# Recurrent attention in steps of 64 tokens of two batches instead of 128 tokens of one, with transposed outputs

## The chip, the cores and the metric

The kernel runs on one NeuronCore of one Trainium2 chip. Four of the core's engines matter here: TensorE (PE in the profile, with the loading of its weights as PEld), VectorE (DVE), ScalarE (ACT) and GpSimd (POOL); SyncE (SP) gives out the DMA transfers. The metric is the device time of one execution in microseconds. The kernel before was timed in three runs: 598.31, 598.85 and 598.88 us, so the median is 598.85 us.

## The reference

A gated linear attention over 4 batches of 8 heads, 768 tokens, with heads of 48 channels, is followed by a feed-forward layer:

```python
for t in range(S):                                    # S = 768
    state = alpha[:, :, t, :, None] * state + einsum('bhd,bhe->bhde', k[:, :, t], v[:, :, t])
    y[:, :, t] = einsum('bhd,bhde->bhe', q[:, :, t], state)
x = y.transpose(0, 2, 1, 3).reshape(B * S, H * D)     # 3072 x 384
h = x @ w_in                                          # 384 x 2048
g = h * erf(softplus(h))
out = g @ w_out                                       # 2048 x 384, result 3072 x 384
```

All data are float32. The state of a head is a 48x48 matrix; row d of it is multiplied by alpha[d] at every token.

## The kernel before

**Tiling.** The 3072 tokens are 24 chunks of 128 tokens, each of one batch, so six chunks follow each other in a batch and hand on the state. Two chunks are a block of 256 tokens, and there are 12 blocks. A chunk goes through the steps ld, a1 to a6, a block through H, L1, L2, E, Z, O and out. Heads are kept in pairs: channels of an even head lie in partitions 0 to 47, those of the odd head of the pair in 64 to 111, and four pairs lie side by side. The 16 partitions behind each head hold fixed filling (ones for alpha, zeros for q and k).

**A chunk.** `ld` (line 130) issues seven DMAs on SP's queue: two each for alpha, k and q, one for v. alpha, k and q go to three fixed tiles, of which there is one set. `a0` (line 139) has ACT look for large alphas. `a1` (line 143) runs four scans on DVE, one for each pair, which give the running product A of alpha within the chunk, and POOL copies its last column to `ae`. `a2` has ACT form 1/A by Ln and Exp, in PSUM, and DVE refine it; `a3` multiplies k by 1/A (K) and q by A (Q). `a4` (line 168) multiplies K by Q on PE, one 48x128x128 product for each of eight heads (`pS`, L174); DVE masks the upper triangle (`sT`, two operations, L180). PE also transposes K (`pn`, L187), and ACT copies that (`kn`). `a5` (line 193) adds up the output `py`: Q times the state T for each pair (L199, where the chunk is not the first of its batch) and the masked scores times v for each head (L205). If the chunk is not the last of its batch, the products of K and v follow (`pu`, L214), and DVE updates T (L224 to L229) by four operations on 64 partitions. `a6` (line 231) turns the output, which has tokens in its partitions, into x, which has channels there: three transposes on PE (`px`, L254), a copy on ACT to `x_hi` (L256) and the rest of float32 on DVE as `x_lo` (L257).

**A block.** `H` (line 259) multiplies x by w_in, 18 matrix products for each half of a group (three for each product of float32 parts: `x_hi` and `x_lo` by `wi_hi`, `x_hi` by `wi_lo`); ACT takes the result out of PSUM twice (L283, L284). `L1`, `L2`, `E` and `Z` compute the activation on ACT and DVE; `O` (line 311) splits it into two parts (L320 to L323) and multiplies by w_out (L331), 12 products for each half of a group; `out` writes 256 rows.

**Weights.** 28 steps `wi` and `wo` load the weights as float64 words, turn these into float32 and split them in two parts, on ACT and DVE (L360 to L368, L343, L344). They are all in the first part of the program.

**What sets the order.** Three lists at the top (START, ORDER, TAIL) give the steps in an order written out by hand: START with the weights and the first chunks, ORDER once for each block in between, TAIL at the end. In ORDER the step `a6_0` ends a block's x, and `H_0_0@1` and `H_0_1@1` come right behind it, ahead of `L2_0`, `L2_1` and the four steps `O_2_0@-1` to `O_3_1@-1`. From the order of the steps the framework's planner makes a fixed sequence of instructions for each engine and for SP's queue: it takes the first instruction in the list's order whose inputs should be there by its own costs, so instructions of neighbouring steps interleave. At run time each engine works its sequence in order.

Buffers: PSUM has four banks for attention (`ps_at`), two for H (`ps_h`) and two for the accumulators.

## Time and profile before

| what | value |
|---|---|
| median of three runs | 598.85 us (598.31 to 598.88) |
| span of the profiled execution, first to last instruction | 594.3 us |
| PE busy | 552.4 us (93%), 4282 products |
| DVE busy | 503.0 us (85%), 769 instructions |
| ACT busy | 485.1 us (82%), 845 instructions |
| POOL busy | 20.9 us (4%), 40 instructions |
| DMA engines, mean over the span | 62 GB/s, 20220 packets |

For the profiled execution the profile gives its span; the time of that execution outside the span is not listed by itself, and the median of the runs is 4.55 us above the span. Busy times of PE overlap within one engine since products are pipelined; the interval from one product's start to the next one's is the price of a product in a row of them. A float32 product stands in the profile as two instructions, each with a weight load of its own; a product of the shortened kind (`x_hi`, `wo_hi` and so on) and a transpose stand as one. In a row of a group, "48\*128 48x128" is rows by columns of the weights, and then partitions by elements of what is streamed.

### The profile page before, as it was taken

What the parts mean: (1) busy time and instruction counts of PE and PEld (TensorE: products, weight loads), DVE (VectorE), ACT (ScalarE), POOL (GpSimd) and SP (SyncE); (2) the same over time, 40 slices, a digit from 0 to 9 for tenths busy, and PEclk for the clock granted to TensorE, in tenths of its full rate; (3) what the DMA queues carried; (4) which work ended last, traced back from release to release, by engine and by line L of the source; (5) the groups of instructions that cost most, each with busy time, mean ns of one, the idle gap of its engine ahead of it and who ended that gap; (6) DMA issues with size and microseconds to landing.
All of it is one profiled execution on the core that took longest, in us unless ns stands there. A gap on an engine that the chain in (4) does not pass through costs nothing.

```text
span 594.3 us, 11033 instructions
## 1 busy us (share of the span) xinstructions
PE 552.4 (93%) x4282; PEld 534.8 (90%) x4282; DVE 503.0 (85%) x769; ACT 485.1 (82%) x845; POOL 20.9 (4%) x40
## 2 busy tenths in 40 slices
PE   0679798999999999999999999999999999999994
PEld 0568787999999999999999999999999999999884
DVE  7899999999999869869779879879779879758780
ACT  4558979698989879889879879889788888889941
POOL 1000110002000000000000000000000000000000
PEclk9999798998999999999999999999999999999998
DMA  6584312313112102112112102112112101000001
GB/s 196 176 290 145 110 55 81 120 54 94 28 41 81 41 26 68 41 29 68 40 28 68 41 28 67 41 39 70 28 35 66 34 28 41 1 1 28 1 27 33
DMA packets 20220, 36.98 MB, mean 62 GB/s; under 512 B 3520, under 2 KB 9664, under 8 KB 20160
## 3 DMA queue, kind: packets, MB, share of 16 engines
q1 hardware_dynamic: 20160, 36.19, 19.9%
q8 instruction: 36, 0.59, 0.4%
q14 instruction: 24, 0.20, 0.1%
HBM read 31.46 MB, written 4.72 MB: 61 GB/s over the span
## 4 chain that ended last, share of the span: by engine, by line
PE 81%; DVE 9%; ACT 6%; DMA 2%; issue 1%; SPq 0%; ACTq 0%; DVEq 0%
PE acc L331 33%; PE ph L272 30%; PE py L205 7%; PE pS L174 4%; PE py L199 3%; PE pu L214 2%; DMA wst<-in_moe_w_in_dram 2%; PE pn L187 1%; PE px L254 1%; DVE hs L309 1%; DVE s L308 1%; DVE A L146 1%; ACT wbuf L360 1%; ACT w L283 1%; DVE wbuf L365 1%
## 5 line engine op out<-in xcount | busy, mean ns | idle before, releaser
L272 PE MATMUL ph<-x_hi,wi_hi 128*128 128x256 f32 x576 | 164.0, 288 | 4.0 <-ACT hs L284 3.4
L272 PE MATMUL ph<-x_lo,wi_hi 128*128 128x256 f32 x576 | 163.4, 284 | 0.4 <-DVE x_lo L257 0.4
L272 PE MATMUL ph<-x_hi,wi_lo 128*128 128x256 f32 x576 | 163.2, 284 | 0.0
L331 PE MATMUL acc<-wo_hi,gh 128*128 128x384 f32 x384 | 134.5, 351 | 3.6 <-DVE gh L320 2.6
L331 PE MATMUL acc<-wo_lo,gh 128*128 128x384 f32 x384 | 131.3, 342 | 0.0
L331 PE MATMUL acc<-wo_hi,gl 128*128 128x384 f32 x384 | 130.0, 344 | 1.2 <-DVE gl L323 1.2
L272 PEld LDWEIGHTS ph<-x_hi,wi_hi 128*128 128x128 f32 x576 | 110.4, 192 | 5.8 <-ACT hs L284 4.2
L272 PEld LDWEIGHTS ph<-x_lo,wi_hi 128*128 128x128 f32 x576 | 110.5, 192 | 0.7 <-DVE x_lo L257 0.7
L272 PEld LDWEIGHTS ph<-x_hi,wi_lo 128*128 128x128 f32 x576 | 110.5, 192 | 0.5 <-DVE wi_lo L344 0.5
L283 ACT ACTIVATE w<-ph 128x512 f32<-128x512 f32 x96 | 57.5, 599 | 46.9 <-PE ph L272 44.0
L297 DVE TENSOR_TENSOR t<-s,w 128x1024 f32<-128x1024 f32 x48 | 58.5, 1219 | 29.4 <-ACT w L291 29.3
L331 PEld LDWEIGHTS acc<-wo_hi,gh 128*128 128x128 f32 x384 | 72.8, 190 | 5.3 <-DVE gh L320 2.6
L331 PEld LDWEIGHTS acc<-wo_hi,gl 128*128 128x128 f32 x384 | 72.2, 190 | 2.6 <-DVE gl L323 2.6
L323 DVE TENSOR_TENSOR gl<-hs,gh 128x512 fp32r<-128x512 f32 x96 | 65.3, 683 | 10.8 <-ACT gh L322 10.3
L331 PEld LDWEIGHTS acc<-wo_lo,gh 128*128 128x128 f32 x384 | 73.2, 191 | 0.0
L205 PE MATMUL py<-raw_v,sT 128*128 128x48 f32 x384 | 57.9, 279 | 5.5 <-DVE sT L180 5.5
L308 DVE TENSOR_TENSOR s<-s,w 128x1024 f32<-128x1024 f32 x48 | 58.2, 1218 | 2.3 <-ACT s L303 2.1
L205 PEld LDWEIGHTS py<-raw_v,sT 128*128 128x128 f32 x384 | 53.8, 203 | 6.8 <-DVE sT L180 6.6
L298 DVE SCALAR_TENSOR_TENSOR w<-t,w 128x1024 f32<-128x1024 f32 x48 | 58.4, 1217 | 0.4
L309 DVE SCALAR_TENSOR_TENSOR hs<-s,hs 128x1024 f32<-128x1024 f32 x48 | 58.2, 1217 | 0.3
L289 ACT ACTIVATE s<-w,fixed 128x1024 f32<-128x1024 f32 x48 | 55.1, 1151 | 0.0
L284 ACT ACTIVATE hs<-ph 128x512 f32<-128x512 f32 x96 | 54.8, 593 | 0.0
(67 smaller groups left out, 834.2 us busy)
## 6 DMA issues: line engine op xcount, KB each, us to landing
wst<-in_moe_w_in_dram SPq DMA_DIRECT2D x12, 512.0 KB, 4.6
wst<-in_moe_w_out_dram SPq DMA_DIRECT2D x16, 384.0 KB, 3.4
raw_a<-in_alpha_dram SPq DMA_DIRECT2D x48, 96.0 KB, 2.2
raw_k<-in_k_dram SPq DMA_DIRECT2D x48, 96.0 KB, 2.2
raw_q<-in_q_dram SPq DMA_DIRECT2D x48, 96.0 KB, 2.2
raw_v<-in_v_dram SPq DMA_DIRECT2D x24, 192.0 KB, 2.4
out_dram<-o SPq DMA_DIRECT2D x24, 192.0 KB, 1.9
```

Of the source, the lines that this page charges most:

```text
L174: nc.tensor.matmul(out=pss[par][:, pair, :], lhsT=self.K[rows, pair, :], rhs=self.Q[rows, pair, :], start=True, stop=True,)
L205: nc.tensor.matmul(out=py[:, h * D : (h + 1) * D], lhsT=self.sT[par][:, pair, :], rhs=vt[:, h, :], start=self.first, stop=self.first or pa ...
L272: nc.tensor.matmul(out=o, lhsT=wt[:, kt, fs], rhs=xt[:, kt, :], start=n == 0, stop=n == 3 * KT - 1)
L283: tab(nc.scalar.activation(w, ph, AF.Exp, accum_out=self.pl.flags[:, n : n + 1]))
L284: nc.scalar.activation(self.hs[g][:, sl], ph, AF.Copy)
L289: tab(nc.scalar.activation(s, w, AF.Ln, bias=bone))
L297: nc.vector.tensor_tensor(out=t, in0=s, in1=w, op=ALU.mult)
L298: nc.vector.scalar_tensor_tensor(out=w, in0=t, scalar=2.0, in1=w, op0=ALU.subtract, op1=ALU.mult)
L308: nc.vector.tensor_tensor(out=s, in0=s, in1=w, op=ALU.mult)
L309: nc.vector.scalar_tensor_tensor(out=h, in0=s, scalar=RT2 / 2, in1=h, op0=ALU.add, op1=ALU.mult)
L323: nc.vector.tensor_tensor(out=gl.rearrange("p a t -> p (a t)"), in0=gg, in1=ghf.bitcast(F32), op=ALU.subtract)
L331: nc.tensor.matmul(out=self.acc[tt][:, :DM], lhsT=gt[:, u, ts], rhs=wt[:, f, :], start=f == 0 and n == 0, stop=f == NF - 1 and n == 2,)
```

## The change

A step (still called a chunk) now takes 64 tokens of two batches: `NI = 2` streams of `TC = 64` tokens. There are still 24 of them, but 12 follow each other for each of two pairs of batches, so 2 of the 24 are the first of a batch and 2 the last (before: 4 and 4). The lists START, ORDER and TAIL are not changed.

- Loads: two sets of tiles for alpha, k and q, and two buffers for v. Four more DMAs for each chunk load v a second time (`vx`), so that the two heads of a pair lie in the two halves of the partitions; each of these moves 64 partitions x 4 x 48 floats. POOL clears `vx`'s last 16 columns.
- `a1`: one scan over all 512 columns. It has to start anew at each of the eight pieces of 64: POOL copies the first factor of each piece to a tile `lower`, clears that factor in the data rows (two memsets, one for each head's 48 partitions), and the scan's second operand (max with `lower`) puts the value back.
- `a2`: 1/A is formed in SBUF, w and K share a tile; the look for large values is made here, on A.
- `a4`: the transposes of K come first. The scores are 16 products of 48x64 by 64, whose results lie in one bank, the even head's in partitions 0 to 63, the odd head's in 64 to 127. One masking operation.
- `a5`: the output comes transposed, channels in partitions: 16 products with the state as weights (48x64) and 16 with `vx` as weights (64x64), in the order state, vx for the even head, then state, vx for the odd head. The products of K and v are 16, of 64 rows and 64 columns, and lie in two banks, one for each stream. T is one tile for both streams; DVE updates it by three operations (one where the chunk is the first: two).
- `a6`: no transposes. Every second chunk, six DMAs on SP's queue move rows from one place of the output tile `xf` to another (the fourth pair's channels fill the 16 partitions behind each head of the other three; `w_in`'s rows are put in the same order on the host), and then one copy on ACT and one subtraction on DVE over 768 columns give `x_hi` and `x_lo`.

```diff
-    for nm, fill in (("a", 1.0), ("q", 0.0), ("k", 0.0)):
-        t = raw.tile([P, NP, P], F32, name=f"raw_{nm}")
-        nc.vector.memset(t, fill)
-        raws.append(t)
+    for n in range(2):
+        ra, rq, rk = (raw.tile([P, NP, NI, TC], F32, name=f"raw_{nm}{n}") for nm in "aqk")
+        for t, fill in ((ra, 1.0), (rq, 0.0), (rk, 0.0)):
+            (nc.vector if n == 0 else nc.gpsimd).memset(t, fill)
+        raws.append((ra, rq, rk))
...
         def ld(self):
-            self.vt = raw.tile([P, H, D], F32, name="raw_v", tag="raw_v")
+            self.vt = raw.tile([P, H * D], F32, name="raw_v", tag="raw_v", bufs=2)
+            self.vx = raw.tile([P, NI * NP * D + HD - D], F32, name="raw_x", tag="raw_x", bufs=2)
+            nc.gpsimd.memset(self.vx[:, NI * NP * D :], 0.0)
...
+            for par in range(2):
+                for i in range(NI):
+                    nc.sync.dma_start(
+                        out=self.vx[par * HD : (par + 1) * HD, i * NP * D : (i + 1) * NP * D].rearrange(
+                            "t (a d) -> t a d", a=NP
+                        ),
+                        in_=v[self.m, self.c, i * TC : (i + 1) * TC, :].rearrange(
+                            "t (a b d) -> t b a d", a=NP, b=2
+                        )[:, par],
+                    )
...
         def a1(self):
+            first = self.ra[:, :, :, 0]
+            nc.gpsimd.tensor_scalar(
+                out=lower[:, :, :, 0], in0=first, scalar1=AMIN, scalar2=None, op0=ALU.max
+            )
+            for par in range(2):
+                nc.gpsimd.memset(first[par * HD : par * HD + D], 0.0)
+            nc.vector.tensor_tensor_scan(
+                out=self.A.rearrange(flat), data0=self.ra.rearrange(flat), data1=lower.rearrange(flat), initial=1.0,
+                op0=ALU.mult, op1=ALU.max,
+            )
...
         def a4(self):
+            ps = ps_at.tile([P, NP * NI, TC], F32, name="pS", tag="at")
             for pair in range(NP):
+                for i in range(NI):
+                    for par in range(2):
+                        rows = slice(par * HD, par * HD + D)
+                        nc.tensor.matmul(
+                            out=ps[par * HD : (par + 1) * HD, pair * NI + i, :],
+                            lhsT=K[rows, pair, i, :], rhs=Q[rows, pair, i, :], start=True, stop=True,
+                        )
...
+        def a5(self, moe):
             for pair in range(NP):
+                for i in range(NI):
+                    at0 = (i * NP + pair) * D
+                    for par in range(2):
+                        o = py[par * HD : (par + 1) * HD, pair * NI + i, :]
+                        if not self.first:
+                            nc.tensor.matmul(
+                                out=o, lhsT=T[par * HD : par * HD + D, at0 : at0 + HD],
+                                rhs=self.Q[par * HD : par * HD + D, pair, i, :], start=True, stop=False,
+                            )
+                        nc.tensor.matmul(
+                            out=o, lhsT=vx[par * HD : (par + 1) * HD, at0 : at0 + HD],
+                            rhs=self.sT[par * HD : (par + 1) * HD, pair * NI + i, :], start=self.first, stop=True,
+                        )
             if not self.last:
+                pu = [ps_at.tile([P, 512], F32, name="pu", tag="at") for _ in range(NI)]
                 for pair in range(NP):
                     for par in range(2):
+                        for i in range(NI):
+                            toks, h = slice(i * TC, (i + 1) * TC), 2 * pair + par
+                            nc.tensor.matmul(
+                                out=pu[i][par * HD : (par + 1) * HD, pair * D : (pair + 1) * D],
+                                lhsT=self.kn[toks, pair, par, :], rhs=vt[toks, h * D : (h + 1) * D],
+                                start=True, stop=True,
+                            )
+            nc.scalar.activation(
+                moe.xf[:, :, :, s, :].rearrange("p a i t -> p (a i) t"), py, AF.Copy,
+            )
...
         def a6(self, moe):
             if self.n % 2 == 0:
-                moe.alloc_x()
-            moe.turn(self.yt.rearrange("p a b d -> p (a b d)"), self.n % 2, ps_at, "at")
+                return
+            for j in range(KT):
+                for par in range(2):
+                    nc.sync.dma_start(
+                        out=xf[par * HD + D : (par + 1) * HD, j, :],
+                        in_=xf[par * HD + j * G : par * HD + (j + 1) * G, NP - 1, :],
+                    )
+            moe.alloc_x()
+            x_hi, x_lo = moe.x
+            nc.scalar.activation(x_hi, xf[:, :KT, :], AF.Copy)
+            nc.vector.tensor_tensor(out=x_lo, in0=xf[:, :KT, :], in1=x_hi.bitcast(F32), op=ALU.subtract)
```

Blocks keep 256 tokens, 128 of each of the two batches, so H, L, E, Z and O are not changed, and `out` writes to two places. The path for inputs that the fast way can't carry (`general`) follows the new layout; no instruction of it stands in the profile before.

More of the change, by code (lines that the diff above doesn't have):

```diff
@@ L193, in a5 @@
[L193 to L211 removed]
+                    nc.sync.dma_start(out=t[par * HD : par * HD + D], in_=src[self.m, self.c, par])
@@ new lines, in a3, with a4 @@
+        def a3(self):
+            flat = "p a i t -> p (a i t)"
+            w = self.K.rearrange(flat)
+            nc.vector.tensor_tensor(out=w, in0=self.rk.rearrange(flat), in1=w, op=ALU.mult)
+            self.Q = at.tile([P, NP, NI, TC], F32, name="Q", tag="Q")
+            nc.vector.tensor_tensor(
+                out=self.Q.rearrange(flat), in0=self.rq.rearrange(flat), in1=self.A.rearrange(flat), op=ALU.mult
+            )
+        def a4(self):
+            K, Q = self.K, self.Q
+            if not self.last:
+                pn = ps_at.tile([P, 512], F32, name="pn", tag="at")
+                for pair in range(NP):
+                    nc.tensor.transpose(
+                        pn[:, pair * P : (pair + 1) * P], K[:, pair].rearrange("p i t -> p (i t)"), ident
+                    )
+                self.kn = at.tile([P, NP, 2, HD], F32, name="kn", tag="kn", bufs=1)
+                nc.scalar.activation(self.kn.rearrange("p a b d -> p (a b d)"), pn, AF.Copy)
+            ps = ps_at.tile([P, NP * NI, TC], F32, name="pS", tag="at")
+            for pair in range(NP):
+                for i in range(NI):
[5 more added lines that the diff above has]
+                        )
+            self.sT = at.tile([P, NP * NI, TC], F32, name="sT", tag="sT", bufs=1)
+            nc.vector.tensor_tensor(
+                out=self.sT, in0=ps, in1=maskn.unsqueeze(1).broadcast_to([P, NP * NI, TC]), op=ALU.mult
+            )
@@ L223, in a5 @@
+            nc.scalar.activation(
+                moe.xf[:, :, :, s, :].rearrange("p a i t -> p (a i) t"), py, AF.Copy,
+            )
+            if not self.last:
+                aeb = self.ae.unsqueeze(3).broadcast_to([P, NI, NP, D])
+                for i in range(NI):
+                    U = pu[i][:, : NP * D].rearrange("p (a d) -> p a d", a=NP)
                     if self.first:
                         nc.vector.scalar_tensor_tensor(
-                            out=Tp, in0=Up, scalar=-1.0, in1=ap, op0=ALU.mult, op1=ALU.mult
+                            out=Tv[:, i], in0=U, scalar=-1.0, in1=aeb[:, i], op0=ALU.mult, op1=ALU.mult
@@ L246, in alloc_x, with order @@
             self.x = (x_hi, x_lo)
+        def order(self, y):
+            t = self.pl.gp.tile([P, KT, 2, HD], F32, name="yo", tag="yo", bufs=1)
+            pairs = y.rearrange("p (a b d) -> p a b d", a=NP, b=2)
+            nc.vector.tensor_copy(out=t[:, :, :, :D], in_=pairs[:, :KT])
+            for j in range(KT):
+                G = HD - D
+                nc.vector.tensor_copy(out=t[:, j, :, D:], in_=pairs[:, NP - 1, :, j * G : (j + 1) * G])
+            return t.rearrange("p j b d -> p (j b d)")
         def turn(self, y, c, pool, tag):
@@ L420, in general @@
                     nc.sync.dma_start(
[L421 removed]
+                        out=part[g, b, bass.ds(c * TC, TC), :, par, :].rearrange("t a e -> a t e"), in_=gy[r : r + NP]
                     )
@@ L452, in gla_moe @@
     new_phase(LNEXP)
-    chunks = [Chunk(n) for n in range(2 * NBLK)]
-    moes = [Moe(i * TB, pools) for i in range(NBLK)]
+    chunks = [Chunk(n) for n in range(NS)]
+    moes = []
+    for n in range(NBLK):
+        m, j = divmod(n, CPB // 2)
+        moes.append(Moe(n, [(m * NI + i) * S + j * P for i in range(NI)], pools))
     def run(order, c0, b0):
@@ L517 @@
     from concourse.bass_utils import run_bass_kernel_spmd as _run
-    nc = _bacc.Bacc("TRN2", target_bir_lowering=False, num_devices=1)
+    nc = _bacc.Bacc("TRN2", target_bir_lowering=False, num_devices=1, dynamic_dma_scratch_size=2048)
     arrays, args = {}, []
     B, H, S, D = inputs["q"].shape
-    P = 128
-    CPB = S // P
+    NI, TC, NP, DM = 2, 64, H // 2, H * D
+    M, C, G = B // NI, S // TC, 64 - D
+    order = [
+        c
+        for j in range(NP - 1)
+        for par in range(2)
+        for c in (
+            *range((2 * j + par) * D, (2 * j + par + 1) * D),
+            *((2 * NP - 2 + par) * D + j * G + z for z in range(G)),
+        )
+    ]
     for name in _INS:
```

180 lines of the change are left out of this document (70 added, 110 removed).

## The prediction

> **What bounds the kernel now.** I read the page's busy times and its chain of waits first, then busy time by stretches, then the chain in order of time.
>
> ```profile
> PE 552.4 (93%) x4282; PEld 534.8 (90%) x4282; DVE 503.0 (85%) x769; ACT 485.1 (82%) x845; POOL 20.9 (4%) x40
> PE 81%; DVE 9%; ACT 6%; DMA 2%; issue 1%; SPq 0%; ACTq 0%; DVEq 0%
> ...
> 0.00:100.00 100.00, 68.73 (x509) 62.20 (x510) 92.27 (x178) 72.51 (x138) 8.89 (x22) 0.95 0.49 152
> 332.50:377.30 44.80, 44.80 (x369) 43.88 (x368) 38.03 (x57) 38.14 (x67) 0.83 (x2) 1.00 0.15 45
> ```
>
> The columns of the last two rows are the stretch, then busy time of PE, PEld, DVE, ACT and POOL, the granted clock, the DMA share and GB/s. Averages mislead: in the first 100 us DVE is the busy one (92 of 100 us, PE 69), and in a block of the middle PE has no gap at all while DVE and ACT stand at 38 of 44.8 us. So a microsecond off PE's work counts from about 100 us on, and a microsecond off DVE before that.
>
> ```profile
> 245.34 1.09 PE pS L174 x16
> ...
> 288.10 1.09 PE pS L174 x16
> ...
> 332.90 1.09 PE pS L174 x16
> 338.81 2.12 PE acc L331 x12
> 340.92 2.14 PE ph L272 x18
> ...
> 377.68 1.09 PE pS L174 x16
> ```
>
> From the chain: a block takes 377.68 - 332.90 = 44.8 us, and one with a last and a first chunk of a batch 288.10 - 245.34 = 42.8 us, so such a boundary saves 2.0 us. H takes 144 x 2.14/18 = 17.1 us of a block and O 96 x 2.12/12 = 17.0 us. Attention has the other 10.7 us, 5.3 us for a chunk, and only this part is changed.
>
> ```profile
> 332.83 1.16 PE L174 MATMUL pS<-Q,K 48*128 48x128 f32 x16
> 333.92 0.66 PE L187 MATMUL pn<-ident,K 128*128 128x128 f32 x4
> 334.33 0.36 PE L272 MATMUL ph<-x_hi,wi_hi 128*128 128x256 f32 x1
> ...
> 342.90 0.36 PE L199 MATMUL py<-T,Q 128*128 128x96 f32 x2
> ...
> 345.61 0.67 PE L214 MATMUL pu<-raw_v,kn 128*64 128x48 f32 x16
> 346.21 0.44 PE L331 MATMUL acc<-wo_hi,gh 128*128 128x384 f32 x1
> ...
> 346.67 0.49 PE L254 MATMUL px<-ident,y 128*128 128x128 f32 x3
> 346.91 0.42 PE L331 MATMUL acc<-wo_hi,gl 128*128 128x384 f32 x1
> ```
>
> From start to start in PE's timeline: scores 1.09 us, transposes of K 0.41, output 2.71, K times v 0.60, transposes of the output 0.24; together 5.05 us.
>
> **PE, part by part.** The new forms are 64x64 and 48x64 weights in quarters of the array; no row shows one. The nearest rows are the weight loads:
>
> ```profile
> 332.83 0.19 PEld L174 LDWEIGHTS pS<-Q,K 48*128 48x128 f32 x2
> 332.83 0.97 PEld L174 LDWEIGHTS pS<-Q,K 48*128 48x128 f32 x16
> 345.02 0.53 PEld L205 LDWEIGHTS py<-raw_v,sT 128*128 128x128 f32 x4
> 345.61 0.55 PEld L214 LDWEIGHTS pu<-raw_v,kn 128*64 128x64 f32 x16
> ...
> L214 PEld LDWEIGHTS pu<-raw_v,kn 128*64 128x64 f32 x320 | 11.7, 146 | 1.2
> ```
>
> Output: 4 loads of 128 columns in 0.53 us, one of which lasts 0.19, so three steps of 0.113 us; that is the pace of the whole group, since only 48 or 96 elements are streamed against each. Scores: 16 loads of 128 columns, 15 steps in 0.97 - 0.19, 0.052 us each: these alternate between the upper and the lower half of the rows, and two go on at once. Their first row says more: two loads start within 0.01 us. The source puts both instructions of the even head's product ahead of the odd head's, and one place needs 0.11 us for each, so the second to start is the odd head's, ahead of its turn. Each half works through a stream of its own. K times v: 64 columns, 15 steps in 0.55 - 0.15 = 0.40, 0.027 us each; with the two halves of the columns in turn that is 0.055 us for a load in one place, half of 0.11 for half the columns.
>
> I take it that quarters too are streams of their own, 0.055 us for an instruction in each. *Scores:* 32 instructions in two quarters, 16 x 0.055 = 0.88; the old 1.09 held 8 x 0.105 = 0.84 and 0.25 of entering and leaving, so 1.13. *Transposes of K:* 0.41 as before, now ahead of the scores. *Output:* 64 instructions in two quarters, 32 x 0.055 = 1.76, and 0.10 for entering: 1.86 for 2.71. Four instructions now follow each other in one quarter, not two. If PE looked ahead by less than that, three of four would be paid in full: 16 x 3 x 0.055 = 2.64, no gain; the loads that overtake speak for the lower value. *K times v:* 32 instructions. In four quarters 8 x 0.055 = 0.44 and 0.16 at the edges, 0.60 as before; if only two run at once, 1.04. I take four, since row halves and column halves are each seen side by side. *Transposes of the output:* 0.24 gone. Sum 4.00, which is 1.05 us less for a chunk.
>
> How many chunks count? The masking stands behind each pair of score groups:
>
> ```profile
> L180 DVE TENSOR_TENSOR sT<-pS,maskn x10: 680/684/692, 21.7 to 92.0; 128x512 f32<-128x512 f32 x10
> L180 DVE TENSOR_TENSOR sT<-pS,maskn x38: 660/680/693, 110.1 to 511.8; 128x512 f32<-128x512 f32 x38
> ```
>
> 5 chunks up to 100 us and 19 after, by two a chunk. 19 x 1.05 = 20.0 us saved. Of this goes back what the batches' edges saved: before, three last and three first chunks after 100 us, 6.0 us; now one first (without the state's products, 0.88) and two last (without 0.41 and 0.60), 2.9 us. That is 3.1 lost, 16.9 us net.
>
> **DVE, ACT and POOL.**
>
> ```profile
> L146 DVE TENSOR_TENSOR_SCAN A<-raw_a,fixed 128x128 f32<-128x128 f32 x96 | 35.1, 406 | 0.0
> L180 DVE TENSOR_TENSOR sT<-pS,maskn 128x512 f32<-128x512 f32 x48 | 30.9, 679 | 0.4 <-PE pS L174 0.4
> L257 DVE TENSOR_TENSOR x_lo<-px,x_hi 128x384 fp32r<-128x384 f32 x24 | 13.4, 557 | 11.3 <-ACT x_hi L256 10.5
> L229 DVE TENSOR_TENSOR T<-T,ae 64x192 f32<-64x192 f32 x32 | 11.3, 353 | 0.8
> L209 ACT ACTIVATE y<-py 128x384 f32<-128x384 f32 x24 | 11.8, 490 | 14.3 <-PE py L205 14.3
> L155 ACT ACTIVATE r<-A 128x512 f32<-128x512 f32 x24 | 14.4, 599 | 1.9 <-DVE A L146 1.9
> 334.62 0.19 POOL L151 COPY ae<-A 128x4 f32<-128x4 f32 x1 [22.56 <-DVE A L146]
> 73.43 3.04 POOL L151 COPY ae<-A 128x4 f32<-128x4 f32 x1 [9.16 <-DVE A L146]
> ```
>
> DVE for a chunk: one masking less, 0.68; four state operations of 0.35 become two of the same length and one of 384 columns (0.56 by `x_lo`'s row), 0.15 less; one scan for four, nothing to 0.2; half of two `x_lo` merged, nothing to 0.1. Together 0.8 to 1.1 us. ACT: the output copy has 512 columns like 1/A's Ln, 0.11 more; the rest is even. In the middle neither is on the path. Up to 100 us, five chunks give 4 to 5.5 us back where DVE waits for nothing. Against this stand three POOL operations ahead of each scan. The copy of 128x4 took 0.19 us beside an easy DVE and 3.04 us in the stretch where DVE was full, but if DVE itself stands waiting for POOL, POOL has it free: 3 x 0.2 to 0.6 for a chunk, at most 3 us over five. The second set of tiles lets POOL begin while the scan before is being used. The four extra DMAs cost SP's queue:
>
> ```profile
> 356.15 0.78 SPq L136 DMA_DIRECT2D raw_a<-in_alpha_dram  x2
> raw_a<-in_alpha_dram SPq DMA_DIRECT2D x48, 96.0 KB, 2.2
> ```
>
> 0.39 us of SP for one, 2.2 us to landing. Five chunks x 4 x 0.39 = 7.8 us of SP in the first 100 us, ahead of weights, partly where nothing waits; loads that waited for the single tiles start earlier. For the start I take 3 us gained, bounds 7 gained and 6 lost.
>
> **The moved step: from output to x.** Before:
>
> ```profile
> 345.71 0.49 ACT L209 ACTIVATE y<-py 128x384 f32<-128x384 f32 x1 [0.95 <-PE py L205]
> 347.19 0.49 ACT L256 ACTIVATE x_hi<-px 128x384 fp32r<-128x384 f32 x1
> 348.05 0.40 PE L272 MATMUL ph<-x_hi,wi_hi 128*128 128x256 f32 x2
> ```
>
> From the end of the output products (345.61) to H on the new x: 2.4 us. Now: copy 0.6, six issues on SP 6 x 0.39 = 2.3, landing 2.2, one copy of 768 columns up to 0.98, handing on 0.4, so 6.5 us, 4 us more in each of 12 blocks. The work that hides it is O of the block before (four steps of 12 products, 8.5 us, behind H in the list), the next chunk's scores, and L2's DVE work. Behind the waiting `x_hi` on ACT stand copies out of PSUM for which PE waits; behind the six DMAs on SP stand the next loads and `out`, which have time. Cover gone altogether: 12 x 4 = 48 us. The planner fills by its own costs, so I take half a microsecond for a block, 6 us.
>
> **Sum.** Against the profiled execution: 594.3 - 16.9 - 3 + 6 = 580.4 us of span; the runs' median is 4.55 us above that span, and so 585 us.
>
> **Rivals.** *Two quarters at a time, or a part of the gain lost among DVE and ACT:* K times v costs 0.44 more, 19 x 0.44 = 8 us, 593. ACT at 38.1 of a block of 43 us would be 89% busy, which leaves waits little room; PE's full rows speak against more than that.
>
> *The wait for x takes over (slower):* with the same PE gain, the block's H stands for the moved rows. It decides from (16.9 + 3)/12 = 1.7 us unfilled in each block; at 2.5 us it costs 30 for my 6, so 609 us. For it: SP gives out six transfers one by one, in a fixed order, and DVE and ACT queue behind. Against it: 8.5 us of O to fill with.
>
> *Quarters take turns (slower):* the quarters of one product pair write to one bank, and in rows 0 to 63 and 64 to 127 nothing shows that two may do so at once; the old scores wrote to two banks. Then scores cost 32 x 0.055 + 0.25 = 2.0 and the output 64 x 0.055 + 0.10 = 3.6, with 0.41 and 0.60 6.6 us, 1.6 more than now: 19 x 1.6 = 30, edges 2.2, so 594.3 + 30 + 2 + 3 + 4.55 = 634 us. Against it: the two column halves of K times v write to one bank, in different partitions, side by side. The Trainium skill's TensorEngine Tiling (Array Packing), section Restrictions and Gotchas, has this rule, that different row tiles cannot access the same PSUM bank at one time; by it the time would be this rival's, and no row here tests it for different partitions.
>
> *The change doesn't do what it says:* a chunk beyond the limits sends everything through the general path, which would run token by token, over 768 x 5 DVE operations of at least 0.35 us, 1.3 ms. The sums of inverse factors run over 64 tokens, not 128, so I give it hardly anything.
>
> **Chances.** Forecast 0.45; two quarters or partial gain 0.22; wait for x 0.22; turns 0.09; general path 0.02. A difference of 0.2% (1.2 us) is about what a measurement of this kernel can tell from no change. Faster: 0.45, 0.19 of the second, 0.01 of the third, 0.65. Same: 0.03 and 0.04, 0.07. Slower 0.28. The range: 585 with the start at its best and the wait hidden, 575; up to the wait at 2.5 us, 610. Outside stand the turns, the general path and the ends. The likeliest case alone: 578 to 592.
>
> **What would show it.** In the changed profile: the weight loads of `pS` and `py` in steps of 0.027 us (0.055 is the third rival), `pu` 32 instructions in 0.6 us (1.0 is the first), no idle PE before H for `x_hi` or `x_lo`, a block of 43 us, and DVE under 85 of the first 100 us. Wrong would be the prediction if PE showed gaps in the middle.

## The result: slower by 3%

The changed kernel takes 616.39 us (612.83 to 618.34, four runs) where the kernel before takes 598.70 (598.31 to 598.88): a ratio of 1.031, 95% interval 1.026 to 1.036. The forecast was 585 us. The profiled execution of the changed kernel has a span of 614.5 us against 594.3, so 20.2 us are to be found; the medians differ by 17.7, since the profiled execution of the kernel before was some 2.7 us faster than its median. Of all executions in this document one, of the kernel f2 below, took 981 us and is not in its ratio. First the page of the changed kernel, its busy times and its chain by engine:

```profile
PE 542.8 (88%) x5914; PEld 517.1 (84%) x5914; DVE 478.5 (78%) x653; ACT 487.1 (79%) x835; POOL 70.7 (12%) x141
...
PE 55%; ACT 18%; DVE 8%; DMA 7%; SPq 6%; issue 3%; POOL 2%; ACTq 0%; DVEq 0%; POOLq 0%
```

PE did lose work, 9.6 us of busy time, but its idle time went from 42 to 72 us, and the chain, 81% PE before, now runs through ACT, DMA and SP's queue for nearly a third of the span. To see where, I cut the span at the second output copy of blocks 3, 9 and 12. ACT's timeline has them, first of the kernel before, then of the changed one (the columns are start and duration in us):

```profile
233.60 0.49 ACT L339 ACTIVATE o<-acc 128x384 f32<-128x384 f32 x1
498.30 0.48 ACT L339 ACTIVATE o<-acc 128x384 f32<-128x384 f32 x1
588.69 0.49 ACT L339 ACTIVATE o<-acc 128x384 f32<-128x384 f32 x1 [1.99 <-DMA out_dram<-o]
```

```profile
241.93 0.49 ACT L403 ACTIVATE o<-acc 128x384 f32<-128x384 f32 x1
512.75 0.49 ACT L403 ACTIVATE o<-acc 128x384 f32<-128x384 f32 x1
608.98 0.49 ACT L403 ACTIVATE o<-acc 128x384 f32<-128x384 f32 x1 [2.28 <-DMA out_dram<-o]
```

The start (to the first of these) is 8.3 us longer, the six blocks of the middle 6.1 (45.14 us each for 44.12), the tail 5.8: all three stages lost.

**The middle.** Busy time of PE, PEld, DVE, ACT and POOL over those six blocks, before and after:

```profile
233.60:498.30 264.70, 264.70 (x2142) 259.26 (x2141) 224.17 (x325) 228.13 (x396) 6.04 (x12) 1.00 0.15 44
```

```profile
241.90:512.70 270.80, 263.74 (x2959) 252.32 (x2957) 210.93 (x267) 227.77 (x390) 30.93 (x56) 0.99 0.20 52
```

PE had no gap before; now it idles 7.06 us in six blocks. Over the same stretches I put the time from each product's end to the next one's end to the later product's tile (all product records of the two traces), which gives PE's ledger for a block:

| us a block | before | after | difference |
|---|---|---|---|
| attention (pS, pn, py, pu, px) | 9.79 | 7.96 | -1.83 |
| H, 144 products | 17.06 | 18.30 | +1.24 |
| O, 96 products | 17.26 | 17.70 | +0.44 |
| idle | 0.00 | 1.18 | +1.18 |
| block | 44.12 | 45.14 | +1.02 |

So attention gave what was hoped for (the forecast's terms make 1.75 us a block here: twelve chunks of 1.05 us, less 2.1 us for the batches' edges, two in these blocks before and one now), and 2.86 us came back in three other rows. Ends of products are modelled in the profile. Counted from start to start instead, attention falls by 1.31, H grows by 1.14 and O by 0.02, with the same idle time: how much of a change between attention and H or O is put to which of them depends on the count, the block doesn't. The chain of the changed kernel over one block shows what PE waits for:

```profile
368.41 0.69 ACT w L347 x2
369.10 0.49 ACT hs L348
369.61 1.28 ACT L122
370.92 0.36 issue
371.29 1.06 ACT s L367
372.37 2.36 DVE s L372 x2
374.73 0.53 DVE T L268 x2
375.25 1.14 DVE hs L373
376.39 0.47 DVE T L270
376.86 0.35 DVE gh L384
377.21 0.14 issue
377.34 0.94 PE acc L395 x4
...
399.47 0.51 PE pu L251 x24
399.98 2.29 PE acc L395 x12
402.27 0.05 issue
402.36 0.56 SPq L280
402.92 0.05 issue
...
405.53 0.35 issue
405.88 1.87 DMA xf<-xf
407.89 0.04 issue
407.94 0.85 ACT x_hi L286
```

In two stretches the chain leaves PE, which works meanwhile on what else there is: 8.9 us of the activation's way through ACT and DVE, called gelu from here on (368.41 to 377.34), and 5.7 us of moves and landing (402.27 to 407.94) with 0.85 us of the copy to x_hi behind. In the kernel before, the chain over one block (346.9 to 392 us) has PE alone; its shares by line:

```profile
by line: PE acc L331 40.9%; PE ph L272 38.2%; PE py L205 7.3%; PE pS L174 4.9%; PE py L199 4.4%; PE px L254 2.0%; PE pu L214 1.3%; PE pn L187 1.3%
```

**The tail.** The same two waits meet here with less to fill them. PE's timeline of the changed kernel, and of that without the moves (e1 below):

```profile
558.57 0.66 PE L395 MATMUL acc<-wo_hi,gh 128*128 128x384 f32 x1 [3.92 <-DVE gh L384]
```

```profile
542.59 0.41 PE L389 MATMUL acc<-wo_hi,gh 128*128 128x384 f32 x1 [0.57 <-ACT o L397]
```

39 products of O run while the last moves are under way (536.9 to 544.3 us in PE's records), and then few are left for gelu: PE stands 3.92 us for it. PE's records tell how many products of O are left when the first H of a block starts. For the last block these are 37 in the kernel before, 9 in the changed one and 32 without the moves; for the three blocks ahead of it 37 to 40, 12 to 14 and 36. So the moves use up the products which lay over gelu before.

**The start.** SP's queue, first of the kernel before, then of the changed one:

```profile
27.73 0.43 SPq L354 DMA_DIRECT2D wst<-in_moe_w_in_dram  x1
...
29.61 0.97 SPq L354 DMA_DIRECT2D wst<-in_moe_w_out_dram  x2
30.67 2.38 SPq L354 DMA_DIRECT2D wst<-in_moe_w_in_dram  x3
```

```profile
7.53 2.63 SPq L155 DMA_DIRECT2D raw_x<-in_v_dram  x4
...
18.07 1.08 SPq L418 DMA_DIRECT2D wst<-in_moe_w_in_dram  x2
...
24.88 3.53 SPq L155 DMA_DIRECT2D raw_x<-in_v_dram  x4
28.45 1.54 SPq L418 DMA_DIRECT2D wst<-in_moe_w_in_dram  x3
33.27 4.40 SPq L280 DMA_DIRECT2D xf<-xf  x6
37.71 1.05 SPq L418 DMA_DIRECT2D wst<-in_moe_w_out_dram  x2
```

Each second load of v holds the queue for 2.5 to 3.5 us, the first moves for 4.4, so that by 33 us 9 of the 28 weights have been given out, where it was 14 before; the next leave at 37.7. This count alone is not the loss: the kernel with one load (f3 below) has also given out 9 by then, the next at 37.15 us, and its start is as short as before. DVE, the engine that set the start, is busy 81.5 of the first 100 us (third busy time) instead of 92; it has less work, and it waits more:

```profile
0.00:100.00 100.00, 54.02 (x755) 49.58 (x757) 81.47 (x140) 63.19 (x121) 23.05 (x54) 0.86 0.60 173
```

When the second block's first H starts, the changed kernel is 9.9 us behind, first before, then after:

```profile
83.24 0.38 PE L272 MATMUL ph<-x_hi,wi_hi 128*128 128x256 f32 x1
```

```profile
93.11 0.57 PE L336 MATMUL ph<-x_hi,wi_hi 128*128 128x256 f32 x2 [2.78 <-ACT x_hi L286]
```

### The profile page after: what moved, and what is told of

Its sections match the earlier page's. It is cut to its first block, busy times and chain, and to the rows that moved or that the text cites. A ratio compares the mean times of both kernels' runs of the same rounds, so it can differ in the third digit from the quotient of the medians.

```text
span 614.5 us, 14576 instructions
## 1 busy us (share of the span) xinstructions
PE 542.8 (88%) x5914; PEld 517.1 (84%) x5914; DVE 478.5 (78%) x653; ACT 487.1 (79%) x835; POOL 70.7 (12%) x141
## 4 chain that ended last, share of the span: by engine, by line
PE 55%; ACT 18%; DVE 8%; DMA 7%; SPq 6%; issue 3%; POOL 2%; ACTq 0%; DVEq 0%; POOLq 0%
PE ph L336 25%; PE acc L395 21%; SPq L280 4%; PE pS L217 3%; DMA xf<-xf 3%; ACT w L347 2%; ACT s L353 2%; PE py L237 2%; PE py L241 2%; ACT hs L348 2%; ACT w L354 2%; ACT s L367 2%; DVE s L372 2%; ACT L122 2%; POOL lower L166 2%
## 5 line engine op out<-in xcount | busy, mean ns | idle before, releaser
L336 PE MATMUL ph<-x_hi,wi_hi 128*128 128x256 f32 x576 | 166.7, 292 | 20.0 <-ACT hs L348 12.1
L336 PE MATMUL ph<-x_lo,wi_hi 128*128 128x256 f32 x576 | 165.8, 289 | 2.2 <-DVE x_lo L287 2.2
L387 DVE TENSOR_TENSOR gl<-hs,gh 128x512 fp32r<-128x512 f32 x96 | 64.8, 684 | 10.8 <-ACT gh L386 10.2
L178 POOL COPY ae<-A 128x8 f32<-128x8 f32 x24 | 39.1, 1630 | 217.3 <-DVE A L173 213.1
L348 ACT ACTIVATE hs<-ph 128x512 f32<-128x512 f32 x96 | 56.6, 592 | 0.0
L386 ACT ACTIVATE gh<-hs 128x512 fp32r<-128x512 f32 x72 | 45.1, 628 | 11.4 <-PE acc L395 11.2
```

Of the source, the lines that this page charges most:

```text
L178: nc.gpsimd.tensor_copy(out=self.ae, in_=self.A[:, :, :, TC - 1].rearrange("p a i -> p i a"))
L336: nc.tensor.matmul(out=o, lhsT=wt[:, kt, fs], rhs=xt[:, kt, :], start=n == 0, stop=n == 3 * KT - 1)
L348: nc.scalar.activation(self.hs[g][:, sl], ph, AF.Copy)
L386: nc.scalar.activation(ghf, gg, AF.Copy)
L387: nc.vector.tensor_tensor(out=gl.rearrange("p a t -> p (a t)"), in0=gg, in1=ghf.bitcast(F32), op=ALU.subtract)
```

## The experiments

The table has all kernels by the same three cuts; times are medians, each ratio is against the kernel before on the same chip. Spans by stage come from one profiled execution each. The kernels ran on several chips, on which the kernel before has medians of 596.6 to 598.7 us, so differences of times between rows can be off by some 2 us. The expectations put f4's block at 43.8 us and e4's at 43.2; by the table's cuts they are 44.20 and 43.50.

| kernel | us | ratio (95%) | start | block | tail |
|---|---|---|---|---|---|
| before | 598.70 | | 233.6 | 44.12 | 90.4 |
| changed | 616.39 | 1.031 (1.026-1.036) | 241.9 | 45.14 | 96.2 |
| e1 no moves | 600.21 | 1.006 (1.004-1.008) | 236.7 | 43.86 | 93.6 |
| e2 no second load | 602.83 | 1.010 (1.007-1.014) | 233.1 | 44.30 | 96.6 |
| e3 restart on DVE | 623.97 | 1.046 (1.042-1.050) | 251.9 | 44.69 | 95.5 |
| e4 all three | 593.16 | 0.992 (0.989-0.995) | 232.2 | 43.50 | 93.1 |
| f1 before, no state products | 595.09 | 0.997 (0.995-1.000) | 239.3 | 42.68 | 93.6 |
| f2 f1 and less of H | 572.23 | 0.960 (0.955-0.964) | 236.6 | 40.05 | 91.1 |
| f3 one packed load | 606.80 | 1.020 (1.016-1.024) | 232.9 | 44.42 | 95.4 |
| f4 f3, moves on two queues | 602.98 | 1.012 (1.008-1.015) | 234.4 | 44.20 | 96.1 |
| g2 moves on GpSimd | 621.32 | 1.037 (1.034-1.041) | 247.3 | 45.07 | 96.2 |
| g4 f4, H earlier in the list | 605.28 | 1.011 (1.007-1.014) | 235.2 | 44.40 | 97.3 |
| g5 f4, x in halves | 619.29 | 1.034 (1.031-1.037) | 240.1 | 45.53 | 99.0 |
| h1 e4, no check of A | 591.80 | 0.993 (0.991-0.996) | 230.9 | 43.77 | 94.1 |
| h2 f4, check on DVE | 599.87 | 1.005 (1.002-1.008) | 231.3 | 44.20 | 95.5 |
| h3 changed, pS twice | 634.72 | 1.065 (1.060-1.069) | 250.1 | 46.67 | 96.4 |
| h4 changed, no state products | 603.85 | 1.014 (1.009-1.019) | 242.2 | 43.07 | 95.5 |
| i1 four loads, longer rows | 618.04 | 1.036 (1.032-1.040) | 243.3 | 44.97 | 96.1 |
| i2 f3, no moves | 596.33 | 0.999 (0.995-1.002) | 230.7 | 43.80 | 93.5 |

**The added parts, one by one.** Without the moves:

```diff
-            for j in range(KT):
-                for par in range(2):
-                    nc.sync.dma_start(out=xf[par * HD + D : ...], in_=xf[...])
```

> The six transfers that move rows of xf at the end of each block are left out, so 96 of the 384 channels of x are wrong; all else is as in the changed kernel (616 us). Theory MOVE (the wait from output to x eats the gain of the middle): blocks fall from 44.9 to about 42.5 us, 9 blocks x 2.4 = 22 us, and some 3 us in the start: 592 us. Theory START (loads and POOL set the first 140 us, and the middle is short of something else, ACT or DVE): blocks stay above 44 us, about 610 us.

Without the second load of v (`py` reads one tile of zeros) and its clearing on POOL:

```diff
-            self.vx = raw.tile([P, ...], F32, name="raw_x", tag="raw_x", bufs=2)
-            nc.gpsimd.memset(self.vx[:, NI * NP * D :], 0.0)
...
-                    nc.sync.dma_start(out=self.vx[...], in_=v[self.m, self.c, ...])
+            self.vx = vx0
```

> The second load of v (four transfers a chunk, 192-byte pieces) and its clearing on POOL are left out; a zero tile stands in, so the output lacks what the chunk's own tokens give. Theory START: SP's queue is freed of 96 issues of about 0.63 us, and the first loads land earlier; the third block's x comes 6 us or more earlier than at 133 us: 606 to 610 us. Theory MOVE: the start gains 2 us at most: 614 us.

With the restart of the scan prepared by DVE:

```diff
-            nc.gpsimd.tensor_scalar(out=lower[:, :, :, 0], in0=first, ...)
+            nc.vector.tensor_scalar(out=lower[:, :, :, 0], in0=first, ...)
...
-                nc.gpsimd.memset(first[par * HD : par * HD + D], 0.0)
+                nc.vector.memset(first[par * HD : par * HD + D], 0.0)
```

> The three operations that prepare the scan's restart (copy of the first factors, two clearings) are done by DVE instead of POOL; the output is complete. DVE gets 72 operations of about 0.1 us. If POOL's starved operation of 9.9 us in the start is what delays the first blocks (theory START), the start loses 6 to 10 us: 607 to 610 us. If the late load of that chunk is the cause, or the middle (theory MOVE): 615 us.

All three at once:

> All three at once: no moved rows, no second load of v, restart prepared on DVE (output wrong as in the two). If the three causes together are the whole difference to the forecast, the forecast's sum without its 6 us for the wait should come out, 580 us (577 to 586), and a block of 42.3 us. If blocks stay above 43.5 us, something else in the middle is missing from my list: 590 us or more.

The moves are worth 16.2 us, spread over all stages (5.2 start, 7.7 middle, 2.6 tail). The second load is worth 13.6, most of it in the start (8.9). Neither theory foresaw these times: e1 lies between the two expectations, e2 below both. All three edits together give 23.2; the restart on DVE alone costs 7.6, so whether the other two overlap can't be told from this. POOL falls as a cause of the start's loss. One of its operations does take 9.88 us in the changed kernel, and the chain runs through it, but in the kernel i1 below the same operation takes 0.52 us, and its start is as long (243.3). POOL's timeline, first of the changed kernel, then of i1:

```profile
50.09 9.88 POOL L166 TENSOR_SCALAR lower<-raw_a 128x8 f32<-128x8 f32 x1 [4.57 <-DMA raw_a<-in_alpha_dram]
```

```profile
51.51 0.52 POOL L160 TENSOR_SCALAR lower<-raw_a 128x8 f32<-128x8 f32 x1 [18.12 <-DMA raw_a<-in_alpha_dram]
```

On DVE the same work makes the start 10 us longer; what it delays there I did not follow up. And e4, expected at 580 us with a block of 42.3, leaves a riddle: with the added waits gone its block is 43.5 us, where attention's 1.83 us off the old block would give 42.3. Its chain is no longer PE's:

```profile
ACT 39%; PE 36%; DVE 16%; issue 4%; DMA 4%; DVEq 0%; ACTq 0%; SPq 0%
```

**Does PE's work set the block at all?** The state's products left out of the kernel before, and then a third of half of H's products as well:

```diff
-                if not self.first:
-                    nc.tensor.matmul(out=py[:, ...], lhsT=self.Q[:, pair, :], rhs=T[...], start=True, stop=False)
...
-                    for wt, xt in ((wi_hi, x_hi), (wi_hi, x_lo), (wi_lo, x_hi)):
+                    for wt, xt in ((wi_hi, x_hi), (wi_hi, x_lo), (wi_lo, x_hi))[: 3 - half]:
```

> The kernel before, with the four products of the state (T and Q into py, L199) left out of each chunk; the output lacks what earlier chunks add. TensorE's work falls by 8 records of 0.109 us a chunk, 1.7 us a block of two chunks, some 15 us over the stretch in which the block repeats. Theory PE (the kernel before is bound by TensorE in its middle, and ScalarE with 38 of 44 us has room): the block falls from 44.1 to about 42.5 us and the time from 598 to 582 to 585. Rival CHAIN (the chain x_hi, H, exponential, logarithms, gelu, output through ScalarE and VectorE is as long as the block already, so that less work on TensorE becomes waiting on it): the block stays at 43.6 or more and the time at 593 or more.

> As the kernel without the state's products, and of the products of H the third of each three (wi_lo with x_hi) left out in the second half of each group as well; the output is less exact. TensorE has 24 products of 0.118 us less in a block, 2.8 us, 4.4 to 4.5 us with the state's. Theory PE: block about 39.7 us, time about 550 to 560. Rival CHAIN: the block stops where the other engines hold it, at 42 us or more, and the time at 580 or more. Where it stops is the bound that my prediction did not have.

The block falls by 1.44 us for 1.53 less attention in the ledger, and by 4.07 for the two cuts of 4.0 together, down to 40.05. So ScalarE and VectorE leave room at 44 us, as the prediction had it. The times miss what theory PE expected: f1's moves by only 1.7 us, since its start is 5.7 us longer and its tail 3.2, and f2's stays above 560. An edit makes the planner put out another sequence, and start and tail can shift by some microseconds with it.

The same cut in the changed kernel, and the opposite, the scores made twice:

```diff
-                        if not self.first:
-                            nc.tensor.matmul(out=o, lhsT=T[...], rhs=self.Q[...], start=True, stop=False)
```

> The changed kernel with the products of the state (T and Q into py, L237) left out; the output lacks what earlier chunks add. The same cut took 1.7 us off the block of the kernel before. Here it is 56 records of 0.031 us, 1.7 us of TensorE a block as well. Theory CHAIN (the block is set by gelu's way through ScalarE and VectorE and by the move of x): block within 0.5 us of 44.6, time 611 or more. Rival PE (the block still follows TensorE): 43.0 us, time about 600.

```diff
-            for pair in range(NP):
+            for pair in [*range(NP), *range(NP)]:
```

> The changed kernel with the products of pS made twice, into the same tile, the second time over the first; the whole output is computed. 1.08 us more of TensorE a chunk, 2.2 us a block. Theory CHAIN: part of it falls into TensorE's idle time, 1.1 us a block, and the slow products after waits: 0.5 to 1.5 us a block, 621 to 630. Rival PE: 2.2 us a block and the start's part, 636 or more.

The theory I held by then, that a chain beside PE sets the block, falls with h4; h3's time and block lie between the two expectations, but by the ledger the block goes down 2.07 us for 1.80 less attention and up 1.53 for 1.71 more. PE's idle time stays where it was, 1.13 and 1.30 us a block. So in these two runs the waits stand in line with PE's work, not beside it: PE saves or loses nearly its time in full, and the waits are added to it.

**Or ScalarE's work?** Without the check of A (1.85 us of ScalarE a block), in the kernel without the added waits; and with that check as a maximum on DVE, whole output, on the kernel with two queues (the edit of the second):

```diff
-            nc.scalar.activation(r, A, AF.Relu, bias=bhi, accum_out=flags[:, self.n, 1:2])
+            nc.vector.tensor_reduce(out=flags[:, self.n, 1:2], in_=A, op=ALU.max, axis=mybir.AxisListType.X)
```

> The kernel with moves and second load left out and the restart on VectorE (593.2, block 43.2), and besides without the check of A against its bound (Relu with its sum, L184: 0.73 and 0.20 us of ScalarE a chunk, 1.85 us a block). Theory CHAIN (in that kernel ScalarE's chain runs without a gap over 28 of 43.8 us): the block falls by 0.7 us (one of the two stands on the chain) to 1.85, to 42.5 or less, and the time to 574 to 585. Rival (another wait takes the place, or TensorE sets the block): within 2 us of 593.

> The kernel with one load of 1600-byte rows and the moves on two queues (603.0, block 43.8), the check of A made by VectorE as a maximum instead of by ScalarE; the whole output is computed. ScalarE has 1.85 us less a block, VectorE about 1.2 us more. Theory CHAIN: 0.5 to 1.5 us a block less, 587 to 598. Rival: VectorE's work stands in the same chain (Z, the updates of T, the scan), and nothing comes of it, 601 or more.

The middle of the one without the check, ACT's busy time (fourth) over six blocks:

```profile
230.90:493.50 262.60, 257.17 (x2957) 246.25 (x2956) 213.48 (x300) 217.89 (x367) 24.01 (x12) 1.00 0.14 42
```

Its blocks are no shorter (43.77 for 43.50) though ACT works 7.7 us less in them (217.89 for 225.59). The amount of ScalarE's work is not the bound. On the other kernel the start gains 3 us, the block nothing; its time, 599.87, lies between the two expectations.

**What makes the second load dear?** One DMA of 128 rows of 1600 bytes, from an input that holds v once more in the wanted order; and the same array in four DMAs:

```diff
-            for par in range(2):
-                for i in range(NI):
-                    nc.sync.dma_start(out=self.vx[...], in_=v[self.m, self.c, ...])
+            nc.sync.dma_start(out=self.vx, in_=vp[self.m, self.c])
```

```diff
+            for par in range(2):
+                for i in range(NI):
+                    nc.sync.dma_start(out=self.vx[rows, cols], in_=vp[self.m, self.c, rows, cols])
```

> The changed kernel, its second load of v as one DMA of 128 rows of 1600 bytes from an array that holds v once more in the order in which it is wanted (four DMAs of 192-byte pieces before), and so no clearing of its last columns on GpSimd. The whole output is computed. Leaving this load out altogether gave 602.8 against 616.4. Theory PIECES (the four issues on SyncE and the small pieces made it dear): 603 to 607. Rival BYTES (that there is a second load of 200 KB a chunk at all): 612 or more.

> The changed kernel with its second load of v from the array that holds v in the wanted order, but still as four DMAs, each of 64 rows of 768 bytes (832 with the empty columns); no clearing on GpSimd. The whole output is computed. One load of 1600-byte rows gave 606.8 (601.9 to 608.7), four of 192-byte pieces 616.4. Theory PIECES (16 times 3,072 packets fewer are what helps): within 2 us of the kernel with one load, which runs beside it in no call, so 603 to 608. Rival ISSUES (SyncE's four times 0.6 us): 612 or more.

The page's DMA line of the changed kernel, of the one with four packed loads, and of the one with a single load:

```profile
DMA packets 48650, 43.09 MB, mean 70 GB/s; under 512 B 30785, under 2 KB 38081, under 8 KB 48577
```

```profile
DMA packets 30217, 43.29 MB, mean 70 GB/s; under 512 B 6208, under 2 KB 19648, under 8 KB 30144
```

```profile
DMA packets 25993, 43.28 MB, mean 72 GB/s; under 512 B 5056, under 2 KB 15424, under 8 KB 25920
```

A clear miss for the pieces: 24,600 small packets fewer bring nothing (618.04), three issues fewer a chunk bring 9.6 us (606.80; its profiled execution is the fastest of five, so its start may flatter it, but leaving the load out says the same). The clearing on POOL is gone in both, so it isn't that either. The table bears this out: among the versions of the new kernel, the start takes 230.7 to 235.2 us with one issue or none and at most six moves a block, and 241.9 or more with four issues and the moves. With one issue two weights behind it leave 5.1 us sooner, in SP's timeline of the kernel with a single load:

```profile
12.56 0.35 SPq L152 DMA_DIRECT2D raw_x<-in_vp_dram  x1
12.95 0.91 SPq L408 DMA_DIRECT2D wst<-in_moe_w_in_dram  x2
```

By which way the issues cost 9 us is not shown. The planner also orders the other engines anew: DVE's sequence differs between f3 and the changed kernel from its 19th instruction on. How much is SP's own time and how much the other sequence was not separated.

**What do the moves cost, and where?** Left out of the kernel with one load; half of them issued by ScalarE; all by GpSimd, in the changed kernel; and made for each chunk, so that x comes in halves:

```diff
-                    nc.sync.dma_start(out=xf[...
+                    (nc.sync if par else nc.scalar).dma_start(out=xf[...
```

```diff
-                    nc.sync.dma_start(out=xf[...
+                    nc.gpsimd.dma_start(out=xf[...
```

```diff
-            if self.n % 2 == 0:
-                return
-            xf = moe.xf.rearrange("p a i s t -> p a (i s t)")
+            s = self.n % 2
+            xf = moe.xf[:, :, :, s, :]
...
```

> The kernel with one load of 1600-byte rows, and the six moves of x left out; rows 48 to 63 of each half of x hold something else, so the output is wrong in what the fourth pair of heads gives. Leaving the moves out took 16.2 us off the changed kernel. Theory SERIAL (the move's 5.6 us stand in line with TensorE once a block and at the end, and only a fill of the output's products covers them): 7 to 12 us less than with the moves, 594 to 599, the tail 3 us shorter and the blocks 0.5 us. Rival SHARED (the moves were dear only because the pieces of the load stood in SyncE's queue with them): within 4 us of the kernel with the moves, 602 or more.

> As the kernel with one load of 1600-byte rows, and three of the six moves of x (those of the lower half) issued by ScalarE instead of SyncE. The whole output is computed. Theory ISSUE (the six issues of 0.62 us in a row on one queue are what the move costs, 3.7 of 7.5 us between the copy to xf and H): 1.9 us off that path; where the path ends the wait, about 0.6 us a block less, 5 to 7 us in all against the kernel with one load. Rival LANDING (the 1.8 us of the transfer and the wait itself are the price, or ScalarE pays for issuing): within 2 us of the kernel with one load, or slower.

> The changed kernel, all six moves of x issued by GpSimd instead of SyncE; the four loads of 192-byte pieces stay. The whole output is computed. Without the moves the time was 600.2, with them on SyncE 616.4. Theory QUEUE (on SyncE the moves wait for the copy to xf, up to 24 us in the start, and every load behind them waits too): most of the 16 us come back, 602 to 608, and the third block's output copy comes at 237 us as without the moves, not at 242. Rival LATENCY (what costs is the way from the copy through the moves to x_hi, whatever the queue): 613 or more, with blocks of 44.5 us as before.

> The kernel with one load of 1600-byte rows and the moves on two queues (603.0), with x made in halves: after each chunk the six moves, the copy to x_hi and the difference x_lo for that chunk's 128 tokens, as the kernel before does, instead of once for 256. The whole output is computed. Twelve moves a block instead of six. Theory PATH (the way from the second chunk's copy to H is what the middle waits for): x_hi takes 0.49 instead of 0.85 us and x_lo 0.55 instead of 0.95 on it, 0.4 to 0.8 us a block, 595 to 599. Rival ISSUES (the queues' time counts, 3.7 us more of it a block): 603 or more.

With a cheap load the moves cost 10.5 us by the medians; of the spans 2.2 in the start, 3.7 in the middle and 1.9 in the tail. Two queues give 3.8 back by the medians, 1.3 of it in the middle, less than expected. GpSimd is worse, and doesn't test what I meant it to, because POOL then stands behind the moves itself:

```profile
POOL xf L280 <- ACT xf L256: 52.6, 11, 38.9
```

The numbers are the wait in all, how often, and the longest: up to 38.9 us, with the preparation of the next scan behind it in POOL's queue. Halves lose 16 us: six moves more a block seem to cost more than shorter copies bring, which fits the load's result, that the number of issues counts.

**The order.** In the repeated list, H of the block ahead of the output's first step:

```diff
-E@-1 Z_0@-1 O_0_0@-1 O_0_1@-1 a1_0 a2_0 Z_1@-1 O_1_0@-1 a3_0 H_1_0 H_1_1 H_2_0
+E@-1 Z_0@-1 H_1_0 O_0_0@-1 O_0_1@-1 a1_0 a2_0 Z_1@-1 H_1_1 O_1_0@-1 a3_0 H_2_0
```

> The kernel with one load of 1600-byte rows and the moves on two queues (603.0), and in the repeated order the first H of a block handed out ahead of the output's first step, the second ahead of the output's third. The whole output is computed. Theory ORDER (TensorE now comes to the output's first products before gelu has been through ScalarE and VectorE, because the order was written for slower attention; with H ahead it has work there): blocks of 43.3 us or less instead of 43.8, 594 to 599. Rival: the planner has H there already, or the wait moves to the next place: 601 or more.

The time is the same within the intervals. No version with the whole output beats the kernel before; the nearest is h2, 0.5% slower (0.2 to 0.8%). Even without the moves and with one load (i2) the time only equals it.

## Why the prediction was wrong

*The size of the miss.* The span was forecast 13.9 us below the kernel before and came out 20.2 above, 34 us apart. About 13 of these lie ahead of the second block's first H (3 gained was the forecast, 9.9 lost the result), 13.6 in the six blocks of the middle (forecast 7.5 less, measured 6.1 more), the rest behind and between.

*What bounds the kernel.* Held for the middle: PE's work counts nearly one for one, in both kernels (f1, h4, h3). The prediction's own sign of being wrong came all the same, gaps of PE in the middle and a block of 45.1 us for 43. For the start it had DVE as the bound; DVE is busy 10.8 us less of the first 100 us now, and nothing is gained.

*PE, part by part.* Held. In blocks without a batch's edge the ledger has 4.13 us a chunk for 5.24 before, 1.11 less where the step had 1.05; from start to start, as the forecast's terms were counted, 4.26 for 5.08, 0.82 less (scores 1.19, transposes of K 0.56 where 0.41 was taken, output 1.85, K times v 0.66). The chain of the changed kernel:

```profile
387.60 1.08 PE pS L217 x32
...
397.46 0.27 PE py L237 x4
397.73 0.12 PE py L241 x4
```

In one row of them the scores take 1.08 us (1.13 forecast), four instructions of the output 0.12 us, the 0.03 us a piece of two streams side by side; in PE's records they start by twos, within 0.01 us of each other. The rival in which the quarters take turns falls, and with it, for this case, the rule in the Trainium skill's TensorEngine Tiling (Array Packing), Restrictions and Gotchas: both row halves of `pS` and `py` write one bank, in different partitions, and by that rule the scores would take 2.0 us, by the prediction's estimate. The measurement decides. Four quarters at once for `pu` held too: in PE's records its 32 instructions start within 0.56 us, by fours, every 0.058 us. So the first rival's two at a time were not it.

*The start.* The step that failed is "The four extra DMAs cost SP's queue": priced at 0.39 us each, "partly where nothing waits", within bounds of 7 gained and 6 lost, and 3 gained taken. By the second block's first H 9.9 us were lost. An issue takes about 0.65 us here (2.63 for four), and above all the bound on what the issues can cost was wrong: leaving the second load out is worth 8.9 us of the start (e2), and replacing its four issues by one about as much (f3 against changed, i1 the control). That it is the weights behind them in the queue is argued, not shown. The forecast that DVE would be under 85 of the first 100 us came true, in part for the wrong reason: DVE also waits more.

*The moved step.* The second failure. From the start of the copy to H it took 7.5 us (the middle one of blocks 4 to 12, 6.6 to 8.1) where 6.5 were added up (six issues of 0.62 us, not 0.39), but its price was "half a microsecond for a block, 6 us", and leaving the moves out is worth 16.2 us (10.5 once the load is cheap), 1.28 us for a block of the middle. The cover I named, O of the block before, does cover the moves; what I did not ask is what that O had covered until then, gelu's way: 37 to 40 of its products were left for that, now 12 to 14, and 9 in the last block. The rival of the wait for x had the right mechanism with its 609 us; its point of decision, 1.7 us unfilled in each block, was not reached by idle time alone (1.18).

*What had no term.* The third failure, and the largest in the middle: that H and O keep their length was taken without a reason, and by the ledger they grew by 1.68 us a block, 10.1 of the 13.6 us. In the records, a full-array product takes about 0.2 us more when it is the first behind attention's products in parts of the array (0.32 for 0.12 in H), and about 0.26 more when it is the first behind idle time (0.39 in H); such first products are 7.5 a block in the changed kernel (4.7 and 2.8) and 2.0 before, all of the first kind. That is some 1.3 us, and H's own step went from 118 to 120 ns, 0.3 us a block.

*The sum.* 4.55 us were put on the span for time outside it. In all 18 kernels profiled since, the same execution's time is 1.6 to 1.9 us above its span, so some 2.8 us of the 4.55 were one execution being faster than the median. And the edges that go back leave out the last chunk of the fourth batch in the kernel before, while they count the new kernel's last one: 1.0 us more should have gone back.

Still open: why a block keeps 0.64 us of idle time and 1.1 us of slower products without moves and with a cheap load (i2), so that of 2.05 us saved in attention 0.3 reach the block. It isn't the amount of ScalarE's work (h1) nor was it cured by one other order (g4); the planner's order as a whole remains as the suspect, for this as for the start, and was not tested.

## What to carry to other kernels

A fill of work that hides a new wait is taken from somewhere: before a wait is put down as hidden, look up in the chain which wait the same work hides today, and what is left at the end of the program, where there is no next block. Count DMAs on an in-order queue by number, not by bytes, above all in a start that loads weights through it. And price a cut in a fully busy engine twice: by the time of its instructions, which came nearly in full here, and by the gaps and switches that the new order puts between the rest.

## What the runs showed of the hardware

- Quarters of the array in rows 0 to 63 and 64 to 127 run side by side although they write one PSUM bank, in different partitions: 0.03 us for an instruction of 64 columns in the changed kernel (`pS`, `py`), 0.015 in four quarters (`pu`, four every 0.058), 0.11 for a load of 128 columns in the whole array in the kernel before (`py`).
- Four DMA issues for one, 24 times, cost some 10 us in this kernel, with the new sequence that comes with them; pieces of 192 instead of 768 bytes cost nothing that can be seen (616.4 and 618.0).
- The step of H's products, the same instructions in all kernels, is 120 ns (median of the records) where the second load of v is made and 117 to 118 where it isn't (before, f1, f2, e2, e4, h1). Why was not looked into.
